# Attention phases merged by pair, one PSUM ring, and weight blocks three in flight: a sigmoid-attention and gated-MLP kernel

## The chip, the cores and the metric

The kernel runs on one core of a Trainium2 chip. It is one launch, and what counts is the device time of that launch in microseconds. Five engines work on it, each with its own instruction queue: TensorE (PE; its weight loads are shown apart as PEld), VectorE (DVE), ScalarE (ACT), GpSimd (POOL) and SyncE (SP), which here only issues transfers. PE writes its results to PSUM, eight banks of 512 fp32 words per partition; ACT and DVE read them from there.

## The reference

Attention with a sigmoid in place of the softmax, over 8 batches, 12 heads, 448 positions, 64 channels, and then a gated MLP with a spatial product, on the heads laid side by side (768 channels):

```python
scores = scale * np.matmul(q, k.transpose(0, 1, 3, 2)) - np.log(S)
attn = 1.0 / (1.0 + np.exp(-scores))
x = np.matmul(attn, v)                      # then heads side by side
h = np.maximum(x @ w_in, 0.0)
u, v = h[..., :d_ff // 2], h[..., d_ff // 2:]
v_n = (v - mean(v)) / np.sqrt(var(v) + 1e-06)
v_s = np.einsum('ts,bsd->btd', w_spatial, v_n) + b_spatial[None, :, None]
return (u * v_s) @ w_out
```

d_ff is 1024, so `u` and `v` have 512 columns. All arrays are float32, but `w_in` and `w_out` reach the chip as 64-bit words, which the kernel converts to fp32 itself.

## The kernel before

**Numbers.** Where precision is needed, an fp32 tile is split into a high and a low part (`split`, L99: a copy to fp32r, then a difference on DVE), and a product is three matmuls (`TERMS`, L217).

**Attention.** A unit is a pair of heads of one batch (`units`, L457: 48), and the loop of `attention` (L470) takes two units, an even and an odd one, called a pair below. The 448 key positions of a unit are three full tiles of 128 and 64 left over; the two leftovers of a pair share one tile, the short one. So a pair has seven tiles of scores: three even, one short, three odd. For each, `attention_scores` (L221) writes scores for two heads into two PSUM banks (`psc`), and ACT makes the sigmoid `at` of them (L254, 128x896). Full tiles have two matmuls side by side, each on half of the rows (64*128, L246); the short one has four on quarters of the array (64*64, L228). `attention_values` (L267) multiplies `at` with `v`, two matmuls side by side, each on half of the columns (128*64, L284), and sums over the tiles of a unit in one PSUM bank (`pav`); then ACT copies the sum to the high part of `x_s` (L290) and DVE makes the low part (L263). In a pair the order on PE is: short scores, even scores, odd values of the pair before, odd scores, even and short values.

**MLP.** For two batches at a time (m = 0 to 3): `gate_values` (`pv`, four groups of sequence tiles), `spatial` (`pg`), `gated` (`pu`), `output` (`po`), in the order of L526 to L554. The first scores of the next two batches stand ahead of the last three `output` calls, and `attention` goes on behind them.

**Memory that is handed round.** PSUM is three pairs of banks (`ps_2`, L82, all of `psc`, `pv`, `pg`, `pu`, `po`) and two single banks (`ps_1`, `pav`). In SBUF, the raw `q` and `k` of units and the weight blocks of the MLP share three buffers (`raw`), the splits three (`split`), `v` three (`v`). A buffer is given out in turn, and whoever takes it waits for its last reader.

**Weights.** `weight_steps` (L141) is a generator: 22 blocks (12 of `w_in`, 4 of `w_spatial`, 6 of `w_out`) are loaded, converted and split, and `load_weights(n)` (L192) runs it up to its n-th next `yield`. At m = 0 calls stand between the other work: the first 13 blocks (`NFIRST`) are done on DVE alone beside the first attention, the other nine in the MLP, by DVE and ACT in turn (sign and clamp on DVE L114 and L121, scaling on ACT L123, two joins on DVE L130 and L133, copy on ACT L178, difference on DVE L182). One block is finished before the next is begun.

**Order.** `in_program_order` (L18) keeps every engine's instructions in the order in which the code writes them, so that the place of a call is its place in each queue.

Of the kernel before, what the change touches and what calls it, by code (L numbers as in the profile page):

```python
# [8 lines left out]
F32 = mybir.dt.float32  # L9
# [5 lines left out]
P = 128  # L15
# [20 lines left out]
def attn_gmlp_kernel(  # L36
# [70 lines left out]
    YB = 4  # L107
    BIG = 7

    def convert(l, raw, scalar):  # L110

        r = raw.rearrange("p (n w) -> p w n", w=2)
        low, a = r[:, 0], r[:, 1]
        nc.vector.tensor_scalar(l, a, 0x80000000, None, op0=ALU.bitwise_and)  # L114


        af = a.bitcast(F32)
        bound = 122879.9921875
        if scalar:

            nc.vector.tensor_scalar(af, af, -bound, bound, op0=ALU.max, op1=ALU.min)  # L121
            yield
            nc.scalar.mul(af, af, 2.0**-112)  # L123
        else:
            nc.vector.tensor_scalar(
                a, a, 1, 1, op0=ALU.logical_shift_left, op1=ALU.logical_shift_right
            )
            nc.vector.tensor_scalar(af, af, bound, 2.0**-112, op0=ALU.min, op1=ALU.mult)
        yield
# [6 lines left out]
        yield  # L136

# [3 lines left out]
    def weight_steps():  # L141
# [8 lines left out]
        def load(n):  # L150
            if n < len(steps):
                src, _, i = steps[n]
                w = 512 if src is w_sp else 1024

                if n < NFIRST:
                    raw = work.tile([P, 1024], U32, tag="tmp", name=f"wraw_{n}", bufs=3)[:, :w]
                else:
                    raw = work.tile([P, 1024], U32, tag="raw", name=f"wraw_{n}", bufs=3)
# [6 lines left out]
        for n, (src, dst, i) in enumerate(steps):  # L165
# [3 lines left out]
            hi, lo = dst[:, i, 0], dst[:, i, 1]  # L169
            scalar = n >= NFIRST  # L170
            val = raws.pop(n)
            if src is not w_sp:
                raw = val
                val = work.tile([P, 512], U32, tag="wval", name=f"wval_{n}", bufs=2)
                yield from convert(val, raw, scalar)
                val = val.bitcast(F32)
            if scalar:
                nc.scalar.copy(hi, val)  # L178
                yield
            else:  # L180
                nc.vector.tensor_copy(hi, val)
            nc.vector.tensor_sub(lo, val, hi.bitcast(F32))  # L182
            if not scalar:
                yield


    NFIRST = NCC + NFC + 3
    NYIELDS = 3 * (NCC + 3) + NFC
# [10 lines left out]
    def attention_loads(b, hp):  # L199
        raw = work.tile([P, 1024], F32, tag="raw", name=f"raw_{b}_{hp}", bufs=3)[:, : 2 * S]  # L200
# [409 lines left out]
```

## Time and profile before

| | us |
|---|---|
| median of three runs | 694.8 (693.76 to 695.07) |
| the profiled execution | 694.26 |
| its span, first to last instruction | 692.5 |
| ACT busy | 249.2 |
| DVE busy | 283.9 |
| POOL busy | 18.5 |

The span is what the profile's rows add up to; the remaining 1.8 us of the execution lie around it. A row of a view has the start, the length, the engine, the line of the kernel, the operation with the tiles written and read, and how many such instructions were merged. A row of the chain of waits has the start, the length and who held the chain then. Mean granted clock of TensorE over the span is 0.997. Busy time by slices (a digit is tenths, 40 slices of 17.3 us):

```
PE   9999999989999999999999999999999999999997
DVE  2999576723243337321324414621224241553020
ACT  7887121322476601011257741010136773101111
```

The slices with ACT at 5 to 8 are the four attentions; those with ACT at 1 to 3 the MLPs between them.

### The profile page before, as it was taken

What the parts mean: (1) busy time and instruction counts of PE and PEld (TensorE: products, weight loads), DVE (VectorE), ACT (ScalarE), POOL (GpSimd) and SP (SyncE); (2) the same over time, 40 slices, a digit from 0 to 9 for tenths busy, and PEclk for the clock granted to TensorE, in tenths of its full rate; (3) what the DMA queues carried; (4) which work ended last, traced back from release to release, by engine and by line L of the source; (5) the groups of instructions that cost most, each with busy time, mean ns of one, the idle gap of its engine ahead of it and who ended that gap; (6) DMA issues with size and microseconds to landing.
All of it is one profiled execution on the core that took longest, in us unless ns stands there. A gap on an engine that the chain in (4) does not pass through costs nothing.

```text
span 692.5 us, 9010 instructions
## 1 busy us (share of the span) xinstructions
PE 684.0 (99%) x3826; PEld 501.9 (72%) x3826; DVE 283.9 (41%) x451; ACT 249.2 (36%) x299; POOL 18.5 (3%) x36
## 2 busy tenths in 40 slices
PE   9999999989999999999999999999999999999997
PEld 3454889978744478999864448899985445889996
DVE  2999576723243337321324414621224241553020
ACT  7887121322476601011257741010136773101111
POOL 0000010000000001000000000100000000110000
PEclk9999999999999999999999999999999999999999
DMA  8683111242243000005332300000433410000102
GB/s 290 224 283 123 31 36 56 87 162 80 86 155 133 1 1 0 1 4 182 107 134 85 129 1 0 1 1 27 160 129 112 158 56 0 1 1 0 54 27 80
DMA packets 20552, 55.37 MB, mean 80 GB/s; under 512 B 1952, under 2 KB 8352, under 8 KB 20512
## 3 DMA queue, kind: packets, MB, share of 16 engines
q1 hardware_dynamic: 20224, 54.57, 22.8%
q8 instruction: 30, 0.49, 0.3%
q10 hardware_dynamic: 288, 0.23, 0.1%
q14 instruction: 10, 0.08, 0.0%
HBM read 43.78 MB, written 11.01 MB: 79 GB/s over the span
## 4 chain that ended last, share of the span: by engine, by line
PE 98%; DVE 1%; ACT 0%; issue 0%; ACTq 0%
PE pav L284 20%; PE po L297 17%; PE pu L297 17%; PE pv L297 17%; PE psc L246 14%; PE pg L297 10%; PE psc L228 3%; PE warm L306 0%; DVE gs L101 0%; DVE g L416 0%; DVE osb L450 0%; ACT osb L448 0%; DVE w_out_s L182 0%; DVE wval L133 0%; DVE wval L130 0%
## 5 line engine op out<-in xcount | busy, mean ns | idle before, releaser
L254 ACT ACTIVATE at<-psc,bias_s 128x896 f32<-128x896 f32 x168 | 156.0, 1008 | 35.4 <-PE psc L228 25.3
L284 PE MATMUL pav<-at,v 128*64 128x448 f32 (+1 forms) x768 | 140.5, 551 | 0.0
L297 PE MATMUL po<-gs,w_out_s 128*128 128x448 f32 x576 | 122.5, 372 | 3.8 <-ACT w_out_s L178 2.5
L297 PEld LDWEIGHTS po<-gs,w_out_s 128*128 128x128 f32 x576 | 108.9, 190 | 16.4 <-ACT w_out_s L178 2.8
L297 PE MATMUL pu<-x_s,w_in_s 128*128 128x448 f32 x576 | 118.0, 365 | 0.0
L297 PE MATMUL pv<-w_in_s,x_s 128*128 128x512 f32 x504 | 115.4, 390 | 0.0
L297 PEld LDWEIGHTS pu<-x_s,w_in_s 128*128 128x128 f32 x576 | 108.2, 188 | 8.6
L297 PEld LDWEIGHTS pv<-w_in_s,x_s 128*128 128x128 f32 x504 | 94.3, 188 | 22.3 <-issue 2.8
L246 PEld LDWEIGHTS psc<-qks 64*128 64x128 f32 x828 | 72.3, 184 | 39.3 <-ACT at L254 17.5
L284 PEld LDWEIGHTS pav<-at,v 128*64 128x64 f32 (+1 forms) x768 | 42.0, 135 | 78.2 <-issue 73.6
L246 PE MATMUL psc<-qks 64*128 64x448 f32 x828 | 97.7, 377 | 0.0
L263 DVE TENSOR_TENSOR x_s<-pav,x_s 128x448 fp32r<-128x448 f32 x48 | 30.0, 624 | 123.3 <-ACT x_s L290 123.2
L297 PE MATMUL pg<-w_sp_s,vn 128*128 128x448 f32 x352 | 72.8, 365 | 0.0
L297 PEld LDWEIGHTS pg<-w_sp_s,vn 128*128 128x128 f32 x352 | 66.0, 187 | 5.8
L454 ACT COPY osb<-po 128x896 f32<-128x896 f32 x23 | 20.9, 908 | 117.3 <-PE po L297 106.7
L416 DVE SCALAR_TENSOR_TENSOR g<-pu,g 128x896 f32<-128x896 f32 x16 | 17.5, 1092 | 92.1 <-PE pu L297 92.1
L101 DVE TENSOR_TENSOR qks<-raw,qks 128x832 fp32r<-128x832 f32 x46 | 46.7, 1024 | 13.0 <-ACT qks L100 11.8
L100 ACT CAST gs<-g 128x896 fp32r<-128x896 f32 x12 | 11.3, 944 | 105.5 <-DVE g L416 105.5
L100 DVE CAST qks<-raw 128x832 fp32r<-128x832 f32 x36 | 21.2, 588 | 66.7 <-PE po L297 35.3
L290 ACT CAST x_s<-pav 128x448 fp32r<-128x448 f32 x48 | 25.6, 533 | 53.9 <-PE pav L284 53.5
L332 ACT ACTIVATE rv<-pv 128x1024 f32<-128x1024 f32 (+1 forms) x16 | 14.6, 915 | 81.4 <-PE pv L297 81.4
L336 DVE BATCH_NORM_STATS2 stats<-rv 128x6 f32<-128x512 f32 x28 | 19.0, 679 | 47.4 <-ACT rv L332 47.4
(41 smaller groups left out, 242.1 us busy)
## 6 DMA issues: line engine op xcount, KB each, us to landing
raw<-qk_dram SPq DMA_DIRECT2D x48, 448.0 KB, 4.3
v<-v_dram SPq DMA_DIRECT2D x24, 448.0 KB, 4.2
out_dram<-osb SPq DMA_DIRECT2D x23, 448.0 KB, 2.6
wraw<-w_in_dram SPq DMA_DIRECT2D x12, 512.0 KB, 4.2
wraw<-w_out_dram SPq DMA_DIRECT2D x6, 512.0 KB, 3.6
wraw<-w_sp_dram SPq DMA_DIRECT2D x4, 256.0 KB, 4.7
b_bc<-b_sp_dram SPq DMA_DIRECT2D x1, 256.0 KB, 5.0
out_dram<-osb ACTq DMA_DIRECT2D x2, 112.0 KB, 1.7
```

The lines of the kernel that those rows point to most:

```text
L100: copy(hi, src)
L101: nc.vector.tensor_sub(lo, src, hi.bitcast(F32))
L228: nc.tensor.matmul(psc[odd * HALF : (odd + 1) * HALF, j, :S], raw[rows, PART:], raw[rows, FULL:PART], start=True, stop=True,)
L246: nc.tensor.matmul(psc[:, j, :S], st[rows, k : k + P], mv[rows, FULL:PART], start=i == 0, stop=i == len(ops) - 1,)
L254: nc.scalar.activation(at, psc[:, :, :S], AF.Sigmoid, bias=bias_s, scale=QK)
L263: nc.vector.tensor_sub(*late.pop(0))
L284: nc.tensor.matmul(pav[heads, :S], vt[rows, t, heads], at[rows, j], start=start, stop=stop)
L290: nc.scalar.copy(x[:, 0], pav)
L297: nc.tensor.matmul(ps, st, mv, start=start and i == 0, stop=stop and i == len(ops) - 1)
L336: nc.vector.bn_stats(stats, rv[:, i])
L416: nc.vector.scalar_tensor_tensor(g, pu[:, :, :S], 0.0, g, op0=ALU.max, op1=ALU.mult)
L454: nc.scalar.copy(osb, po[:, :, :S])
```

## The change

Four things change.

1. In `attention`, a pair has one phase of scores (short, even, odd) and one of values (even, odd, short); the values of a pair no longer reach into the next one. Both units of a pair end at the short tile, and the four instructions that bring them to `x_s` stand together: two copies on ACT, then two differences on DVE.
2. PSUM becomes one ring of four pairs of banks; `pav` takes one bank of a pair for each of the two units.
3. Weights: 11 blocks in the attention instead of 13. The other eleven are worked on in three parts (`begin`: sign, clamp, scaling; `middle`: two joins, copy; the difference), and the parts of three blocks are interleaved. Of the calls of `load_weights` in the MLP the ones behind the `output` phases go, and earlier ones run more steps.
4. Buffers: `raw` four instead of three, `v` two instead of three, `wval` three instead of two; the loads of `q` and `k` are issued a unit earlier.

```diff
-    ps_2 = ctx.enter_context(tc.tile_pool(name="ps_2", bufs=3, space=bass.MemoryType.PSUM))
-    ps_1 = ctx.enter_context(tc.tile_pool(name="ps_1", bufs=2, space=bass.MemoryType.PSUM))
+    ps_2 = ctx.enter_context(tc.tile_pool(name="ps_2", bufs=4, space=bass.MemoryType.PSUM))
...
+        def begin(n):
+            low, a = words(raws.pop(n))
+            l = value(n)
+            sign(l, a)
+            a = a.bitcast(F32)
+            nc.vector.tensor_scalar(a, a, -BOUND, BOUND, op0=ALU.max, op1=ALU.min)
+            nc.scalar.mul(a, a, SCALE)
+            return l, low, a.bitcast(U32)
+
+        def middle(n, l, low, a):
+            join(l, low, a)
+            nc.scalar.copy(parts(n)[0], l.bitcast(F32))
+            return l.bitcast(F32)
+
+        begun, joined = {}, {}
+        for n in range(NFIRST, len(steps) + 2):
+            load(n + AHEAD)
+            if n < len(steps):
+                begun[n] = begin(n)
+            if n - 2 in joined:
+                hi, lo = parts(n - 2)
+                nc.vector.tensor_sub(lo, joined.pop(n - 2), hi.bitcast(F32))
+            yield
+            if n - 1 in begun:
+                joined[n - 1] = middle(n - 1, *begun.pop(n - 1))
+            yield
...
-    NFIRST = NCC + NFC + 3
-    NYIELDS = 3 * (NCC + 3) + NFC
+    NFIRST = NCC + NFC + 1
+    NYIELDS = 3 * (NCC + 1) + NFC
...
-    def attention_values(b, hp, t, at):
+    def attention_values(b, hp, ats):
         vt = values[b, hp]
...
+        pav = banks(f"pav_{b}_{hp}")
+        evens, odds = range(NFULL), range(NFULL + 1, TILES)
+        for t in (*evens, *odds, NFULL):
+            at = ats(t)
...
+                    nc.tensor.matmul(
+                        pav[heads, odd, :S],
+                        vt[rows, t, heads],
+                        at[rows, j],
+                        start=t == odd * (NFULL + 1),
+                        stop=t == NFULL,
+                    )
+        cols = slice((b % 2) * S, (b % 2 + 1) * S)
+        parts = [(x_s[:, :, hp + odd, cols], pav[:, odd, :S]) for odd in range(2)]
+        for x, ps in parts:
+            nc.scalar.copy(x[:, 0], ps)
+        for x, ps in parts:
+            nc.vector.tensor_sub(x[:, 1], ps, x[:, 0].bitcast(F32))
...
-        load_weights(2 * (n - 1))
+        load_weights(1 if ts[0] else 5)
...
-            if i == 0:
-                load_weights(n - 1)
...
-        load_weights(YB * (b % 2))
+        load_weights(2)
...
         nc.vector.scalar_tensor_tensor(g, pu[:, :, :S], 0.0, g, op0=ALU.max, op1=ALU.mult)
-        load_weights(1)
...
         ahead(attention_loads, n + 2)
+        ahead(attention_loads, n + 3)
...
         for n in range(first, end, 2):
...
+            if n:
+                scores(n, short + evens)
+            else:
+                scores(n, evens)
...
+            if n and n == first:
+                yield
+                attention_splits(*units[n + 1])
+            if n:
+                loads()
+            scores(n, odds)
+            if not n:
+                scores(n, short)
+            weigh(WEIGH + (n + 2 == end))
+            if not n:
+                loads()
             ahead(attention_splits, n + 2, end)
             ahead(attention_splits, n + 3, end)
-            vals(n, evens + short)
-            weigh(3 + (n + 2 == end))
-        vals(end - 2, odds)
+            attention_values(*units[n], lambda t: ats.pop((n, t)))
...
         output(b0, (0, 1))
-        load_weights(YB)
         output(b0, (2, 3))
-        load_weights(YB + 1)
         start_loads(m + 1)
```

`WEIGH` is 4. `value(n)` takes a buffer `wval`, `words(raw)` the two 32-bit halves of the 64-bit words, `sign` and `join` are the passes of the old `convert`.

**PE in the middle of the second attention** (batch 3, the pair of heads 2 and 3; a name is the tile, the batch, the head pair and, for scores, the key tile: 0 to 2 even, 3 short, 4 to 6 odd). Before, from the even scores on:

```order
L246 MATMUL psc_3_2_0_1858<-qks_3_2_1827 128x448 x6
L246 MATMUL psc_3_2_1_1867<-qks_3_2_1827 128x448 x6
L246 MATMUL psc_3_2_2_1876<-qks_3_2_1827 128x448 x6
L284 MATMUL pav_3_1_1842<-at_3_0_4_1807,v_3_0_1666 64x448 x2
L284 MATMUL pav_3_1_1842<-at_3_0_5_1816,v_3_0_1666 64x448 x2
L284 MATMUL pav_3_1_1842<-at_3_0_6_1825,v_3_0_1666 64x448 x2
L246 MATMUL psc_3_2_4_1893<-qks_3_3_1830 128x448 x6
L246 MATMUL psc_3_2_5_1902<-qks_3_3_1830 128x448 x6
L246 MATMUL psc_3_2_6_1911<-qks_3_3_1830 128x448 x6
L284 MATMUL pav_3_2_1926<-at_3_2_0_1865,v_3_2_1761 64x448 x2
L284 MATMUL pav_3_2_1926<-at_3_2_1_1874,v_3_2_1761 64x448 x2
L284 MATMUL pav_3_2_1926<-at_3_2_2_1883,v_3_2_1761 64x448 x2
```

PE in the changed kernel, at the same place:

```order
L269 MATMUL psc_3_2_0_1851<-qks_3_2_1817 128x448 x6
L269 MATMUL psc_3_2_1_1860<-qks_3_2_1817 128x448 x6
L269 MATMUL psc_3_2_2_1869<-qks_3_2_1817 128x448 x6
L269 MATMUL psc_3_2_4_1880<-qks_3_3_1820 128x448 x6
L269 MATMUL psc_3_2_5_1889<-qks_3_3_1820 128x448 x6
L269 MATMUL psc_3_2_6_1898<-qks_3_3_1820 128x448 x6
L295 MATMUL pav_3_2_1913<-at_3_2_0_1858,v_3_2_1784 64x448 x2
L295 MATMUL pav_3_2_1913<-at_3_2_1_1867,v_3_2_1784 64x448 x2
L295 MATMUL pav_3_2_1913<-at_3_2_2_1876,v_3_2_1784 64x448 x2
L295 MATMUL pav_3_2_1913<-at_3_2_4_1887,v_3_2_1784 64x448 x2
L295 MATMUL pav_3_2_1913<-at_3_2_5_1896,v_3_2_1784 64x448 x2
L295 MATMUL pav_3_2_1913<-at_3_2_6_1905,v_3_2_1784 64x448 x2
```

The odd values of the pair before have left their place between the even and the odd scores, and each pair's odd values stand behind its even ones.

**ACT at the same place,** from the last sigmoid of the pair before on. Before:

```order
L254 ACTIVATE at_3_0_6_1825<-psc_3_0_6_1818,bias_s_72 128x2x448
L290 CAST x_s_71<-pav_3_0_1833 128x448
L254 ACTIVATE at_3_2_3_1852<-psc_3_2_3_1847,bias_s_72 128x2x448
L254 ACTIVATE at_3_2_0_1865<-psc_3_2_0_1858,bias_s_72 128x2x448
L254 ACTIVATE at_3_2_1_1874<-psc_3_2_1_1867,bias_s_72 128x2x448
L254 ACTIVATE at_3_2_2_1883<-psc_3_2_2_1876,bias_s_72 128x2x448
L290 CAST x_s_71<-pav_3_1_1842 128x448
L254 ACTIVATE at_3_2_4_1900<-psc_3_2_4_1893,bias_s_72 128x2x448
```

ACT in the changed kernel:

```order
L277 ACTIVATE at_3_0_6_1815<-psc_3_0_6_1808,bias_s_69 128x2x448
L305 CAST x_s_68<-pav_3_0_1823 128x448 x2
L277 ACTIVATE at_3_2_3_1849<-psc_3_2_3_1844,bias_s_69 128x2x448
L277 ACTIVATE at_3_2_0_1858<-psc_3_2_0_1851,bias_s_69 128x2x448
L277 ACTIVATE at_3_2_1_1867<-psc_3_2_1_1860,bias_s_69 128x2x448
L277 ACTIVATE at_3_2_2_1876<-psc_3_2_2_1869,bias_s_69 128x2x448
L277 ACTIVATE at_3_2_4_1887<-psc_3_2_4_1880,bias_s_69 128x2x448
```

Both copies to `x_s` now stand ahead of the short tile's sigmoid, and none between the even and the odd ones.

**ACT in the MLP of m = 0,** from the second `gated` of b = 0 to its `output` copies (L454 before; `wraw_19` and `wval_19` are parts of block 19 of the weights). Before:

```order
L100 CAST gs_0_2_1120<-g_0_2_1020 128x896
L178 CAST w_out_s_68<-wval_17_1113 128x512
L123 ACTIVATE wraw_18_1060<-wraw_18_1060 128x512
L178 CAST w_out_s_68<-wval_18_1150 128x512
L123 ACTIVATE wraw_19_1111<-wraw_19_1111 128x512
L178 CAST w_out_s_68<-wval_19_1185 128x512
L454 COPY osb_0_0_1195<-po_0_0_1194 128x2x448
L123 ACTIVATE wraw_20_1148<-wraw_20_1148 128x512
L178 CAST w_out_s_68<-wval_20_1223 128x512
L454 COPY osb_0_2_1231<-po_0_2_1230 128x2x448
L123 ACTIVATE wraw_21_1183<-wraw_21_1183 128x512
L178 CAST w_out_s_68<-wval_21_1259 128x512
```

ACT in the changed kernel:

```order
L98 CAST gs_0_2_1136<-g_0_2_1034 128x896
L188 ACTIVATE wraw_21_1076<-wraw_21_1076 128x512
L193 CAST w_out_s_65<-wval_20_1127 128x512
L193 CAST w_out_s_65<-wval_21_1139 128x512
L467 COPY osb_0_0_1203<-po_0_0_1202 128x2x448
L467 COPY osb_0_2_1231<-po_0_2_1230 128x2x448
L467 COPY osb_0_4_1269<-po_0_4_1268 128x2x448
```

The last two blocks, 20 and 21, stood between the copies of the first batch's `output` phases; now all weights stand ahead of the first of them.

More of the change, by code (lines that the diff above doesn't have):

```diff
@@ L135, in convert @@
         )
-        yield
     AHEAD = 2
@@ L157, in load @@
                 else:
-                    raw = work.tile([P, 1024], U32, tag="raw", name=f"wraw_{n}", bufs=3)
+                    raw = work.tile([P, 1024], U32, tag="raw", name=f"wraw_{n}", bufs=4)
                 raws[n] = raw.bitcast(F32) if src is w_sp else raw
@@ L164, in weight_steps, with value, parts @@
         yield
-        for n, (src, dst, i) in enumerate(steps):
+        def value(n):
+            return work.tile([P, 512], U32, tag="wval", name=f"wval_{n}", bufs=3)
+        def parts(n):
+            _, dst, i = steps[n]
+            return dst[:, i, 0], dst[:, i, 1]
+        for n, (src, dst, i) in enumerate(steps[:NFIRST]):
             load(n + AHEAD)
@@ L199, in attention_loads @@
     def attention_loads(b, hp):
-        raw = work.tile([P, 1024], F32, tag="raw", name=f"raw_{b}_{hp}", bufs=3)[:, : 2 * S]
+        raw = work.tile([P, 1024], F32, tag="raw", name=f"raw_{b}_{hp}", bufs=4)[:, : 2 * S]
         nc.sync.dma_start(raw, qk[b, hp])
@@ L204, in value_loads @@
     def value_loads(b, hp):
-        vt = work.tile([P, 2 * NFULL + 1, P], F32, tag="v", name=f"v_{b}_{hp}", bufs=3)
+        vt = work.tile([P, 2 * NFULL + 1, P], F32, tag="v", name=f"v_{b}_{hp}", bufs=2)
         nc.sync.dma_start(vt, v[b, hp // 2])
@@ L255, in attention_scores @@
         return at
-    pav_of = {}
-    late = []
-    def late_splits():
-        while late:
-            nc.vector.tensor_sub(*late.pop(0))
-    last = (NFULL, TILES - 1)
-    def attention_values(b, hp, t, at):
-        vt = values[b, hp]
-        for odd in range(2):
-            if t == NFULL:
-                rows = slice(odd * HALF, (odd + 1) * HALF)
-            elif (t > NFULL) == odd:
-                rows = slice(0, P)
-            else:
-                continue
-            unit = b, hp + odd
-            start = t == odd * NFULL
-            stop = t == last[odd]
-            if start:
-                pav_of[unit] = ps_1.tile([P, 512], F32, tag="ps1", name=f"pav_{b}_{hp + odd}")
-            pav = pav_of[unit]
-            for j in range(2):
-                heads = slice(j * D, (j + 1) * D)
-                nc.tensor.matmul(pav[heads, :S], vt[rows, t, heads], at[rows, j], start=start, stop=stop)
-        for odd in range(2):
-            if t == last[odd]:
-                sl = slice((b % 2) * S, (b % 2 + 1) * S)
-                x = x_s[:, :, hp + odd, sl]
-                pav = pav_of.pop((b, hp + odd))[:, :S]
-                nc.scalar.copy(x[:, 0], pav)
-                late.append((x[:, 1], pav, x[:, 0].bitcast(F32)))
```

78 lines of the change are left out of this document (31 added, 47 removed).

## The prediction

> **What bounds the kernel now.** I read the head of the page, then the chain of waits in order of time, then the timeline of one pair of units, and last the busy times by stage.
>
> ```profile
> PE 684.0 (99%) x3826; PEld 501.9 (72%) x3826; DVE 283.9 (41%) x451; ACT 249.2 (36%) x299; POOL 18.5 (3%) x36
> PE 98%; DVE 1%; ACT 0%; issue 0%; ACTq 0%
> ```
>
> TensorE (PE) is busy 684.0 of 692.5 us and carries 98% of the chain that ended last. So an edit pays only where it shortens PE's own sequence or removes one of the few gaps. The largest gap is in the chain of waits, in the MLP of the first batch pair (m = 0), where the first `output` phase meets weights that are not converted yet. The last row is the same phase at m = 1:
>
> ```profile
> 130.49 9.87 PE po L297 x48
> ...
> 141.23 0.66 ACT wraw L123
> ...
> 141.91 0.70 DVE wval L130
> ...
> 144.02 0.70 DVE w_out_s L182
> ...
> 144.76 5.28 PE po L297 x17
> ...
> 304.64 14.78 PE po L297 x72
> ```
>
> The reader is to see one block of `w_out` going from ACT to DVE and on, one step after the other, while PE stands. The phase takes from 130.49 to 144.76 + 5.28 = 150.04, so 19.55 us, against 14.78 for the same matmuls later: **4.77 us lost**. The second place is attention, which has the same beat all through. One period of it:
>
> ```profile
> 24.47 0.75 PE psc L228 x8
> 25.22 2.09 PE psc L246 x18
> 27.31 2.41 PE pav L284 x12
> 29.71 2.02 PE psc L246 x18
> 31.73 3.32 PE pav L284 x20
> 35.05 0.75 PE psc L228 x8
> ```
>
> 35.05 - 24.47 = 10.58 us for a pair of units: short scores, even scores, odd values of the pair before, odd scores, even and short values. PE never stops, but it changes its tile shape at every border, and the borders cost something:
>
> ```profile
> 214.90 1.58 PE L246 MATMUL psc<-qks 64*128 64x448 f32 x14
> 216.11 0.36 PE L246 MATMUL psc<-qks 64*128 64x448 f32 x2
> ```
>
> These are rows of PE's timeline, cut so that it begins at two different matmuls of one scores phase. Two matmuls side by side make a step; six steps lie between the two starts, so a step of scores is (216.11 - 214.90) / 6 = 0.202 us. A step of the 64-column kind is 0.75 / 2 = 0.375, from the short scores above, whose eight matmuls run four abreast; values step at the same beat. The scores phase of 18 matmuls has 9 steps, 1.82 us, and takes 2.02: 0.20 for going in and out. The values phase of 12 has 6 steps, 2.25, and takes 2.41: 0.16.
>
> **The change part by part.**
>
> *Merging the phases.* A pair now has one scores phase and one values phase, so one entry and exit of each goes: 0.20 + 0.16 = 0.36 us. In the first pair of each attention the scores stay cut in two by the outputs, so five borders of six go: 5 x 0.36 = 1.8 us for each m. The number of matmuls does not change.
>
> *The new wait.* The values' accumulator now lies in the ring of four pairs of banks. Per pair the ring gives out eight: short, three even, three odd, values. So values gets the banks of the third even tile, and the next pair's third even tile gets those of values. These are free only when both copies (ACT) and both differences (DVE) have read them, and both units end together, at the short tile. Rows for this, 209.02 being the start of the short scores:
>
> ```profile
> 209.02 0.93 PE L228 MATMUL psc<-raw 64*64 64x448 f32 x8
> 209.24 0.53 ACT L290 CAST x_s<-pav 128x448 fp32r<-128x448 f32 x1 [1.66 <-PE pav L284]
> 209.80 0.62 DVE L263 TENSOR_TENSOR x_s<-pav,x_s 128x448 fp32r<-128x448 f32 x1 [1.57 <-ACT x_s L290]
> 210.11 3.70 ACT L254 ACTIVATE at<-psc,bias_s 128x896 f32<-128x896 f32 x4 [0.34 <-PE psc L228]
> 211.17 0.50 PEld L246 LDWEIGHTS psc<-qks 64*128 64x128 f32 x6 [0.18 <-ACT at L254]
> 33.30 1.68 ACT L100 CAST qks<-raw 128x832 fp32r<-128x832 f32 x2
> 24.10 1.95 DVE L101 TENSOR_TENSOR qks<-raw,qks 128x832 fp32r<-128x832 f32 x2
> ```
>
> Counted from the short scores: first copy at 0.22. The last two rows bound what two alike behind each other do: two casts of about 0.90 take 1.68, two differences of 1.02 take 1.95, so they overlap by about 0.1. Second copy from 0.65 to 1.18; the first difference stands behind both copies (one event is counted for the two), from 1.21, the second ends at about 1.21 + 0.54 + 0.62 = 2.37, and PE can load its weights 0.05 later, at 2.42. In the profile before, the third even tile's weights load at 211.17 - 209.02 = 2.15. **So PE waits 0.28 us** that it does not wait now. Bounds: nothing, if the banks come free by 2.15; with no overlap anywhere and twice the event delays 0.22 + 1.06 + 0.10 + 1.24 + 0.10 = 2.72, so 0.57. I take 0.28, since each piece has a row of its own.
>
> Net, per merged pair: 0.36 - 0.28 = 0.08 us; 20 of them, 1.6 us. The end of each attention gains about 0.1 more, since the odd values of the last pair no longer stand as a phase of their own behind the short ones: 0.4. Attention: **-2.0 us**, between 20 x 0.36 = 7.2 gained and 20 x 0.21 = 4.2 lost.
>
> *ACT's place.* Seven tiles now arrive in a row, one in 0.6 us, and ACT clears one in 3.70 / 4 = 0.92 (0.90 start to start). Its first sigmoid moves from 1.09 to about 1.12, behind the second copy. Odd tile k waits for sigmoid k, and these end at 2.1, 3.0, 3.9 where PE wants the banks at 3.0, 3.6, 4.2. Values wait for the fourth sigmoid, which ends at 1.12 + 3 x 0.90 + 1.01 = 4.83; PE is there at 5.0. So ACT hides, by 0.2 us. Were the wait of 0.28 not there, ACT would hold PE at about 4.9 and give back 0.15 of the gain.
>
> A rule speaks against this part. The Trainium skill, "TensorEngine Tiling (Array Packing)", section Performance Considerations, says that tiling speeds up TensorE but not the evacuation of PSUM, whose copies may become the bottleneck. The trace bears it out in that ACT's 0.90 a tile is slower than PE's 0.6 in this phase; it would bind PE only by the 0.15 just given, and over a whole period ACT has time.
>
> ```profile
> 5.00:69.20 64.20, 64.20 (x445) 29.83 (x441) 52.68 (x92) 52.62 (x63) 0.00 (x0) 1.00 0.66 231
> 69.20:98.00 28.80, 28.80 (x129) 23.86 (x128) 17.44 (x35) 5.98 (x9) 2.32 (x4) 1.00 0.12 37
> 98.00:107.10 9.10, 9.10 (x46) 8.25 (x45) 7.42 (x16) 1.74 (x3) 2.26 (x4) 1.00 0.21 59
> 107.10:121.70 14.60, 14.60 (x74) 13.54 (x73) 9.21 (x14) 2.90 (x4) 0.00 (x0) 1.00 0.11 36
> 121.70:130.50 8.80, 8.80 (x45) 8.26 (x45) 7.89 (x12) 2.85 (x4) 0.00 (x0) 1.00 0.26 73
> 130.50:150.00 19.50, 16.78 (x73) 14.69 (x73) 10.91 (x18) 5.46 (x8) 0.00 (x0) 0.91 0.46 164
> 182.60:243.40 60.80, 60.80 (x432) 29.44 (x431) 20.71 (x29) 42.01 (x50) 0.00 (x0) 1.00 0.26 91
> ```
>
> These are busy times by stage: length, then PE, weight loads, DVE, ACT, POOL, granted clock, DMA share, GB/s. In attention ACT has 42.0 of 60.8 us, and in the first attention 52.6 of 64.2, so it catches up within the period.
>
> *Weights at m = 0.* Two blocks fewer are converted during the first attention, where DVE has 52.7 of 64.2 us; that frees it and moves nothing on PE. Eleven instead of nine are converted in the MLP, each begun two calls before it is finished, so that the round from DVE to ACT and back lies beside other work, and the last is finished ahead of the first `output`. On DVE a block costs two short passes, two joins and one difference:
>
> ```profile
> L114 DVE TENSOR_SCALAR wval<-wraw 128x512 uint32<-128x512 uint32 x18 | 7.6, 424 | 0.0
> L121 DVE TENSOR_SCALAR wraw<-wraw 128x512 f32<-128x512 f32 x9 | 3.9, 431 | 0.3
> ```
>
> 0.42 + 0.43 + 3 x 0.70 = 2.95 us. Between 69.2 and 130.5 DVE is busy 17.44 + 7.42 + 9.21 + 7.89 = 42.0 of 61.3 us, with about six and a half blocks in it. With all eleven it would be 42.0 + 4.5 x 2.95 = 55.3. That fits, but with 6 us to spare. In DVE's own order the split of the second `gated` of b = 0, which the first `output` reads after its sixth matmul, then ends about 1 us before PE wants it; the last two blocks have 10 us more, since only the third `output` reads them. So I count **the whole 4.77 us as gone**, with 0.5 to 2.5 returning if DVE slips by its spare. What hides the conversions is PE's 61.3 us of products.
>
> *The rest.* Loads of `q` and `k` come a unit earlier and with four buffers instead of three; values have two buffers instead of three. Transfers land 4.2 to 4.3 us after issue by the page's list of DMA issues, and each is issued about 10 us or more ahead of its reader, so I cost it at nothing; uncovered, a late `v` would hold the values phase and also the two raw loads behind it on SP's queue.
>
> **Sum,** against the profiled execution's own time of 694.26 us (span 692.5; the median of the runs shown is 694.8, half a microsecond above): 694.26 - 4.77 - 2.0 = **687.5 us**.
>
> **The rivals.** (A) The banks come free in time, because copies and differences go faster than I add up. Then ACT's 0.15 is the only loss: 20 x 0.21 = 4.2 in place of 1.6, 684.9 us. For it: the overlaps of 0.1 us are read off longer instructions. Against: DVE cannot start before 1.2. (B) The release takes its upper bound, or DVE slips in the MLP: 20 x 0.2 lost in place of 2.0 gained, or 2.5 us returned, 690 to 692. For it: 6 us of spare on an engine that waits for ACT in between. (C) The weights do not come in time after all, so that the change does not do what it says: attention alone is left, 692.3. Against: the last block stands ahead of the `output` in the order. (D) Slower: DVE reaches the two differences late, because the splits of the next units stand ahead of them in its queue and wait for a late transfer. Each us then costs PE a us in every period. From 0.35 us late the 20 periods eat all gains (20 x 0.35 = 7); at 0.8 late 16 us are lost, 703. Against: 20.7 of 60.8 us are DVE's, and it is free at about 5.6 of 10.6. (E) PE's new short waits lower its clock. In the profile 0.91 of the clock was granted in the stage with 4 us of gap (130.50 to 150.00), 1.00 where PE waited 0.18 in each period, so I hold it for unlikely; with 3.4 us at half clock in each of 20 periods it would be 20 x 1.7 = 34 us more, about 721. The Trainium skill, "TensorE: Matmul & The Clock Gate", section "A second HAM failure mode: psum-queue depth-cycling", tells of such a loss from small idle times between groups; no run here shows it so far.
>
> **How the numbers follow.** Forecast 0.50 (686 to 689.5), A 0.20 (683 to 686), B 0.18 (689.5 to 692.5), C and whatever else ends near no change 0.05, D 0.05, E 0.02. The range leaves out D, E, C and the far ends of A and B: 683.0 to 691.5. A measurement of this kernel can tell about 0.2% (1.4 us) from no change: faster 0.88, same 0.05, slower 0.07.
>
> **What would show it.** The first `output` at m = 0 should take 14.8 us without a gap, and the clock stay at 1.00 there. A period of attention should be 10.5 us, with PE's weight load for the third even tile waiting about 0.3 us on the difference of `x_s`. The forecast is wrong if that wait is over 0.6 us, if the values phase waits for a sigmoid, or if PE waits in the m = 0 MLP for `gs` or a weight block.

## The result, and the profile after

| | before | changed |
|---|---|---|
| median | 694.49 us (693.76 to 695.07, four runs) | 690.64 us (690.43 to 690.91, four runs) |
| the profiled execution, its span | 694.26, 692.5 | 690.91, 689.1 |
| mean granted clock | 0.997 | 1.000 |

The ratio of the changed kernel to the one before is 0.9945, with a 95% interval of 0.9928 to 0.9963: it is faster, by 3.4 us between the spans and 3.9 between the medians. The forecast was 687.5 us, 6.8 below the profiled execution. The time is inside the range (683.0 to 691.5), but in the band of rival B (689.5 to 692.5) and not in that of the forecast.

(One execution of a kernel below, the profiled one of *attn*, ran at a granted clock of 0.752 over its whole span and took 843.09 us; it is compared with nothing, and *attn_again* is a second profile of that kernel.)

The head of the page, and the share of the engines in the chain that ended last, after the change:

```profile
PE 677.9 (98%) x3826; PEld 508.2 (74%) x3826; DVE 280.6 (41%) x447; ACT 245.8 (36%) x303; POOL 18.5 (3%) x36
PE 92%; DVE 4%; ACT 3%; issue 1%
```

PE's busy time fell by 6.1 us, the span by 3.4 only. DVE and ACT, which had 1% of the chain together, now have 7%: PE has less to do and waits more. The chain of waits of the changed kernel (start, length, who held it), at the second pair of m = 0, at the first `output` phase, and over one period of the second attention:

```profile
15.50 0.98 ACT x_s L305 x2
16.48 1.95 DVE qks L99 x2
18.43 1.08 DVE x_s L307 x2
...
27.99 0.98 ACT x_s L305 x2
...
70.51 28.80 PE pv L313 x126
...
131.78 14.78 PE po L313 x72
...
208.06 0.98 ACT x_s L305 x2
...
209.06 1.17 DVE x_s L307 x2
210.23 0.14 issue
210.36 2.70 PE psc L269 x24
213.06 5.62 PE pav L295 x32
...
218.71 0.98 ACT x_s L305 x2
```

Four things are to be seen. The first `output` phase takes 14.78 us, where it took 19.55. A period of attention is 218.71 - 208.06 = 10.65 us, where it was 10.58. In every period the chain leaves PE for the two copies on ACT and the two differences on DVE, and comes back to PE at the scores. And the first product `pv` of m = 0 starts at 70.51, where it started at 69.23 (the end of the window of the first attention, 69.20, in the prediction). So the account by stages is: -4.77 in the first `output`, +1.28 in the first attention; in each later m, the stretch from the first odd scores to `pv` is 0.17 longer (60.91 after 60.74), and the one ahead of it, from the first short scores over the last `output` calls to the odd scores, 0.11 shorter (17.91 after 18.02), so 3 x 0.06. The sum is -3.3 us, for -3.4 measured between the spans.

The timeline of one pair in the changed kernel (the number in brackets is idle time ahead, with what ended it), with the short scores starting at 218.46:

```profile
218.46 0.93 PE L251 MATMUL psc<-raw 64*64 64x448 f32 x8
...
219.71 1.16 DVE L307 TENSOR_TENSOR x_s<-pav,x_s 128x448 fp32r<-128x448 f32 x2 [6.37 <-ACT x_s L305]
...
220.98 2.39 PEld L269 LDWEIGHTS psc<-qks 64*128 64x128 f32 x24 [0.56 <-PE psc L269]
221.01 2.74 PE L269 MATMUL psc<-qks 64*128 64x448 f32 x24 [0.21 <-DVE x_s L307]
```

The second difference ends at 219.71 + 1.16 = 220.87, 2.41 us after the short scores began, and the weights of the third even tile are loaded at 220.98, 2.52 after. The prediction had 2.37 and 2.42.

Two stages by windows (columns as in the prediction: length, PE, weight loads, DVE, ACT, POOL, clock, DMA share, GB/s), the first `output` and the second attention:

```profile
131.70:146.60 14.90, 14.90 (x75) 13.62 (x74) 6.63 (x10) 3.65 (x5) 0.00 (x0) 1.00 0.29 91
179.10:239.90 60.80, 59.78 (x431) 31.21 (x431) 19.61 (x28) 39.92 (x49) 0.00 (x0) 1.00 0.32 107
```

PE is busy all through the first `output`, at full clock. In the second attention it has 1.0 us of idle time that the same stretch did not have before (60.80 of 60.80). That is less than the periods lose, because the rows of the last matmuls ahead of a wait reach into it (idle 0.21 us above); the periods are the better measure.

**The second pair of m = 0** was not in the prediction. The first weight instruction on DVE, and then the rows of PE:

```profile
11.48 0.43 DVE L116 TENSOR_SCALAR wval<-wraw 128x512 uint32<-128x512 uint32 x1 [10.30 <-DMA wraw<-w_in_dram]
```

```profile
17.55 1.28 PE L269 MATMUL psc<-qks 64*128 64x448 f32 x10 [0.97 <-DVE qks L99]
19.64 2.71 PE L269 MATMUL psc<-qks 64*128 64x448 f32 x24 [0.81 <-DVE x_s L307]
```

DVE waits 10.3 us for the first weight block, has nine instructions on weights from 11.48 on, and only at 16.48 (in the chain above) makes the low parts of the second pair's `q` and `k`, and after these, at 18.43, the differences that free the banks. The block had been issued at 3.04, so 8.4 us passed until it was read; the page's median for such a block was 4.2 us before and is 5.8 us now. PE is idle for 0.97 us at the even scores and for 0.81 at the third even tile, and this pair takes 27.99 - 15.50 = 12.49 us instead of 10.65. In the kernel before, DVE's order at this place was the other way round:

```profile
12.94 1.96 DVE L101 TENSOR_TENSOR qks<-raw,qks 128x832 fp32r<-128x832 f32 x2 [11.77 <-ACT qks L100]
...
15.35 0.42 DVE L114 TENSOR_SCALAR wval<-wraw 128x512 uint32<-128x512 uint32 x1
```

The splits stood ahead of the weights and were done at 14.90. The change had moved the first call of `weigh` past them.

### The profile page after: what moved, and what is told of

Read it like the earlier page. It is cut to its first block, busy times and chain, and to the rows that moved or that the text cites. A ratio compares the mean times of both kernels' runs of the same rounds, so it can differ in the third digit from the quotient of the medians.

```text
span 689.1 us, 9062 instructions
## 1 busy us (share of the span) xinstructions
PE 677.9 (98%) x3826; PEld 508.2 (74%) x3826; DVE 280.6 (41%) x447; ACT 245.8 (36%) x303; POOL 18.5 (3%) x36
## 4 chain that ended last, share of the span: by engine, by line
PE 92%; DVE 4%; ACT 3%; issue 1%
PE pav L295 20%; PE pu L313 17%; PE po L313 17%; PE pv L313 17%; PE pg L313 10%; PE psc L269 10%; DVE x_s L307 3%; ACT x_s L305 3%; PE psc L251 1%; PE warm L322 0%; DVE qks L99 0%; DVE gs L99 0%; DVE g L430 0%; DVE osb L463 0%; ACT osb L461 0%
## 5 line engine op out<-in xcount | busy, mean ns | idle before, releaser
L277 ACT ACTIVATE at<-psc,bias_s 128x896 f32<-128x896 f32 x168 | 154.3, 1032 | 23.0 <-PE psc L251 18.6
L295 PE MATMUL pav<-at,v 128*64 128x448 f32 (+1 forms) x768 | 135.4, 548 | 0.0
L313 PE MATMUL po<-gs,w_out_s 128*128 128x448 f32 x576 | 120.4, 368 | 1.0 <-DVE osb L463 0.9
L295 PEld LDWEIGHTS pav<-at,v 128*64 128x64 f32 (+1 forms) x768 | 44.2, 135 | 80.5 <-issue 73.3
L269 PEld LDWEIGHTS psc<-qks 64*128 64x128 f32 x828 | 77.8, 184 | 31.9 <-PE psc L269 11.6
L307 DVE TENSOR_TENSOR x_s<-pav,x_s 128x448 fp32r<-128x448 f32 x48 | 27.8, 620 | 135.8 <-ACT x_s L305 135.8
L305 ACT CAST x_s<-pav 128x448 fp32r<-128x448 f32 x48 | 23.2, 536 | 76.0 <-PE pav L295 76.0
```

The costliest lines, as they stand in the source:

```text
L269: nc.tensor.matmul(psc[:, j, :S], st[rows, k : k + P], mv[rows, FULL:PART], start=i == 0, stop=i == len(ops) - 1,)
L277: nc.scalar.activation(at, psc[:, :, :S], AF.Sigmoid, bias=bias_s, scale=QK)
L295: nc.tensor.matmul(pav[heads, odd, :S], vt[rows, t, heads], at[rows, j], start=t == odd * (NFULL + 1), stop=t == NFULL,)
L305: nc.scalar.copy(x[:, 0], ps)
L307: nc.vector.tensor_sub(x[:, 1], ps, x[:, 0].bitcast(F32))
L313: nc.tensor.matmul(ps, st, mv, start=start and i == 0, stop=stop and i == len(ops) - 1)
```

## The experiments

The theory after reading the two traces: the weight part takes away exactly the 4.77 us of the first `output`; merging the phases saves what was predicted, but the new wait for the banks that the copies and differences free eats all of it; and in m = 0 a burst of weight conversions ahead of the splits costs about 2 us more. Rivals: the sigmoids on ACT hold PE, not the banks; the borders between phases are worth less than counted; the loss in m = 0 comes from the loads.

All ratios are to the kernel before, measured beside it on the same chip; its medians were 693.78 to 694.49 us. Medians of two rows can come from different chips, so tenths between them mean little; where a tenth matters, it is read from the profiles.

| run | what | median, us | ratio, 95% interval |
|---|---|---|---|
| the change | | 690.64 | 0.9945 (0.9928 to 0.9963) |
| weights | before + weight part | 689.83 | 0.9939 (0.9925 to 0.9952) |
| attn | change without weight part | 696.59 | 1.0036 (1.0024 to 1.0048) |
| attn_again | the same | 698.25 | 1.0061 (1.0042 to 1.0079) |
| staged | change, banks freed by one ACT copy | 684.94 | 0.9868 (0.9855 to 0.9882) |
| onecopy | change, one copy and one difference | 686.67 | 0.9892 (0.9878 to 0.9907) |
| inter | change, copy, difference, copy, difference | 700.78 | 1.0096 (1.0081 to 1.0111) |
| twopools | change, PSUM pools of before | 700.04 | 1.0084 (1.0069 to 1.0099) |
| wlate | change, first weight call moved | 692.03 | 0.9971 (0.9959 to 0.9982) |
| behind1 | change, all weight calls moved | 689.55 | 0.9933 (0.9919 to 0.9946) |
| behind | staged and behind1 together | 683.83 | 0.9853 (0.9837 to 0.9870) |

### The two halves of the change: weights, attn, attn_again

*weights* is the kernel before with the new `weight_steps`, the calls of `load_weights` as in the change, and its buffers. In the attention the places of the calls stay, with other counts, and the loads of `q` and `k` are issued where they were before:

```diff
-                weigh(3)
+                weigh(2)
...
-            weigh(3 + (n + 2 == end))
+            weigh((4 if n < 2 else 2) + (n + 2 == end))
```

> The kernel before with the weight part of the change alone (three blocks in flight, two blocks fewer in the first attention, four raw buffers, two value buffers); phases and PSUM pools as before. If the 4.77 us in the first output phase are all that the weight part is worth: 694.3 - 4.8 = 689.5 us, the first output phase 14.8 us at clock 1.00. Rival: the weight part also costs time in the first attention, because its first block now stands ahead of the splits of the second pair in DVE's order: then 690.5 to 691.5, and the values of m=0 start up to 1.3 us later than before. If the merged phases were the source of the whole gain, 694.

Its chain of waits in m = 0:

```profile
19.11 6.63 DMA raw<-qk_dram
...
70.83 28.79 PE pv L322 x126
...
132.09 14.78 PE po L322 x72
```

689.83 us, 0.6% faster. The first `output` takes 14.78 us, as in the change. The rival's 1.3 us in the first attention is there too (`pv` at 70.83 instead of 69.23), but not for its reason: DVE makes the second pair's splits at 13.03, ahead of the weights, and the chain goes through a load of `q` and `k` that was issued only at 19.11, behind a weight load that went out at 18.26. In this mix, then, a load is late that the change, which issues these loads a unit earlier, has in time. So in the profiled execution, the slowest of the five (690.67), 4.8 us were gained and 1.6 lost again.

*attn* is the changed kernel with the old `weight_steps`, its calls, and 13 blocks in the first attention.

```diff
-    WEIGH = 4
+    WEIGH = 5
...
-    NFIRST = NCC + NFC + 1
+    NFIRST = NCC + NFC + 3
```

> The changed kernel with the old weight code (one phase of scores and one of values per pair, ring of four pairs of banks; weights converted as before). If the wait for the banks eats what a merge saves (about 0.45 us of wait against 0.36 saved), attention is no faster than before: 690.7 + 4.8 = 695.5 us, so 0.1 to 0.3% slower than before, the gap of 4.8 us back in the first output phase. By the prediction's sum (wait 0.28): 692.3. If the mode changes were dearer than counted and the m=0 loss comes from the new weight code: 691 to 692.

696.59 us, slower than before by 0.24 to 0.48%. The merged phases and the ring alone do not pay; by the prediction's sum they should have given 2.0 us. It is 1.1 us above the 695.5 expected, and where that lies is asked of a second profile:

> The same kernel as in the run attn (the change without its weight part), for a profile of its stages. attn took 696.6 where 690.7 + 4.8 = 695.5 was expected, 1.1 more. If the missing 1.1 lies in the first attention (two more weight blocks in DVE's bursts ahead of the splits): values of m=0 to the first product 71.5 to 72 us where the changed kernel has 70.5, the first output phase 19.5, the attentions of m of 1 to 3 as in the changed kernel, 60.9 from the odd scores to the product. Rival: the first output phase alone loses more (20.6), or the attentions of m of 1 to 3 do.

```profile
43.19 8.11 DMA wraw<-w_in_dram
...
73.44 28.76 PE pv L289 x126
...
134.67 9.87 PE po L289 x48
...
148.96 5.29 PE po L289 x17
```

The first `output` runs from 134.67 to 154.25, 19.58 us, so no more is lost there than before. `pv` starts at 73.44, 2.9 later than in the changed kernel and 1.4 later than the expectation allowed. The span of this execution is 696.8, 7.7 above the changed kernel's: 2.9 + 4.8. In this execution the extra lies in the first attention alone, and here the chain goes through a weight block that landed late, with the splits and the differences behind it in DVE's queue. It is an execution of 698.56 us; the five of *attn* took 695.74 to 697.00, so where the 1.1 us of *attn* lie is not shown by it, and why the same program took 1.7 us more the second time stays open.

### The wait for the banks: staged, onecopy, inter

*staged* frees the banks with one instruction in m = 1 to 3; in m = 0 it has one copy and one difference for the pair:

```diff
-        parts = [(x_s[:, :, hp + odd, cols], pav[:, odd, :S]) for odd in range(2)]
-        for x, ps in parts:
+        x, ps = x_s[:, :, hp : hp + 2, cols], pav[:, :, :S]
+        if b > 1:
+            o = work.tile([P, 2, 512], F32, tag="tmp", name=f"o_{b}_{hp}", bufs=3)[:, :, :S]
+            nc.scalar.copy(o, ps)
+            split(x[:, 0], x[:, 1], o, nc.vector.tensor_copy)
+        else:
             nc.scalar.copy(x[:, 0], ps)
-        for x, ps in parts:
             nc.vector.tensor_sub(x[:, 1], ps, x[:, 0].bitcast(F32))
```

> The changed kernel, but ACT copies values' accumulator of both units in one instruction of 128x896 to SBUF for m of 1 to 3, and DVE makes both parts from there, so that the banks are free after one ACT copy; for m=0 one copy and one difference of 128x896. If the chain of two copies and two differences sets the third even tile: that tile no longer waits, the copy ends about 1.1 us after the short scores' start instead of 2.4, and a period of m of 1 to 3 goes from 10.65 to 10.2 to 10.3 us (ACT then holds PE by 0.1): 15 such periods, 5 to 6 us less, 685 us. Rival 1: ACT's sigmoids hold PE anyway (values wait for the fourth): period 10.5 or more, 688.5 or more. Rival 2: the wait is no loss, because PE catches up in it what it loses elsewhere: no change, 690.5.

A period of it in the chain of waits:

```profile
195.96 0.75 PE psc L251 x8
196.72 3.90 PE psc L269 x36
...
200.63 5.64 PE pav L295 x32
206.28 0.75 PE psc L251 x8
```

684.94 us, as the theory had it. The chain stays on PE: the 36 scores take 3.90 in one piece, and a period is 206.28 - 195.96 = 10.32 us. Values are 5.57 long where nothing holds them (the rows of *onecopy* next), so up to 0.1 of the period is ACT holding PE at the values, and the bare period is 0.75 + 3.90 + 5.57 = 10.22. This gives both terms of the sum apart, to a few hundredths, since it adds rounded rows. **A merged pair without a wait is 10.58 - 10.22 = 0.36 us shorter than before**, the prediction's value. **The wait for the banks costs 10.65 - 10.22 = 0.43**, against 0.28 predicted.

Two more readings are needed to say what is in these numbers. One is when the weight load of the third even tile starts where nothing holds it. In *staged*, with the short scores at 206.09:

```profile
206.09 0.93 PE L251 MATMUL psc<-raw 64*64 64x448 f32 x8
...
206.96 3.58 PEld L269 LDWEIGHTS psc<-qks 64*128 64x128 f32 x36 [0.71 <-PE pav L295]
```

The 36 loads of the scores run through without a gap, six to a tile; the 13th, the first of the third even tile, starts at 208.08, 1.99 us after the short scores. In the kernel before it was 2.15, because there the load was itself held 0.18 us for a sigmoid (the row at 211.17 in the prediction). The other is that this small wait costs PE about 0.08 us a period in the kernel before: its even scores take 2.10 us, but 2.02 in the first pair of the second attention, which has no such wait:

```profile
165.54 2.02 PE psc L246 x18
```

*onecopy* shortens the chain without leaving it:

```diff
-        for x, ps in parts:
-            nc.scalar.copy(x[:, 0], ps)
-        for x, ps in parts:
-            nc.vector.tensor_sub(x[:, 1], ps, x[:, 0].bitcast(F32))
+        x, ps = x_s[:, :, hp : hp + 2, cols], pav[:, :, :S]
+        nc.scalar.copy(x[:, 0], ps)
+        nc.vector.tensor_sub(x[:, 1], ps, x[:, 0].bitcast(F32))
```

> The changed kernel with one copy and one difference of 128x896 per pair in place of two of 128x448 each. If the third even tile waits for the end of this chain: the copy takes 0.91 and the difference 1.09 in one piece against two that overlap by 0.1, with one wait between engines as before; the banks are free 2.25 us after the short scores' start instead of 2.41, so 0.15 us less per pair: 15 pairs of m of 1 to 3 give 2.3, and m=0 gains the 1.0 us that the kernel with the SBUF copy showed there with this form: 687.4 us. Rival: the wait is set by something else at that place (the sigmoid of the short scores, which moves earlier by little): 689.9 to 690.6.

Its chain over one period, and its timeline, with the short scores at 206.68:

```profile
196.40 0.75 PE psc L251 x8
...
201.28 5.57 PE pav L295 x32
206.86 0.75 PE psc L251 x8
```

```profile
207.86 1.09 DVE L305 TENSOR_TENSOR x_s<-pav,x_s 128x896 fp32r<-128x896 f32 x1 [6.24 <-ACT x_s L304]
...
209.01 2.33 PEld L269 LDWEIGHTS psc<-qks 64*128 64x128 f32 x24 [0.36 <-DVE x_s L305]
```

686.67 us, 0.7 better than expected. The chain ends at 207.86 + 1.09 = 208.95, 2.27 after the short scores' start; the 0.14 gained there was expected (2.25). The rest was not: the weights load 0.06 after the difference ends, where in the change they load 0.11 after it. So a period is 206.86 - 196.40 = 10.46 us, 0.19 less than the change's, and not 0.15 (over all periods of m = 1 to 3 the means are 10.44 and 10.66).

*inter* lengthens the chain, by deleting one line:

```diff
         for x, ps in parts:
             nc.scalar.copy(x[:, 0], ps)
-        for x, ps in parts:
             nc.vector.tensor_sub(x[:, 1], ps, x[:, 0].bitcast(F32))
```

> The changed kernel with copy, difference, copy, difference in this order in place of two copies and two differences; nothing else. If the chain that frees the banks sets the third even tile, it now runs one step after the other: banks free 2.63 us after the short scores' start or later instead of 2.41, and the sigmoid of the short scores moves from 1.1 to 1.9: 0.2 to 0.45 us more in each of 21 periods, 695 to 700 us. Rival: PE waits there for something else, or the time is made up later in the period: 690.6.

```profile
189.51 0.54 ACT x_s L305
...
191.94 0.14 issue
192.07 2.83 PE psc L269 x24
194.92 5.69 PE pav L295 x32
200.63 0.54 ACT x_s L305
```

700.78 us, 10 more than the change, a little over the expected end. The four steps (only the first is shown) now run strictly one after the other, 191.94 - 189.51 = 2.43 us instead of 210.23 - 208.06 = 2.17. A period is 200.63 - 189.51 = 11.12, so 0.47 more than the change: 0.26 is the chain, and 0.20 the scores and values behind it (2.83 + 5.69 instead of 2.70 + 5.62), which fits that the sigmoids start later too. With a shorter chain, a longer chain, and none, PE's time follows the chain each time; that the banks set the third even tile is shown.

### What the fourth pair of banks is for: twopools

```diff
-    ps_2 = ctx.enter_context(tc.tile_pool(name="ps_2", bufs=4, space=bass.MemoryType.PSUM))
+    ps_2 = ctx.enter_context(tc.tile_pool(name="ps_2", bufs=3, space=bass.MemoryType.PSUM))
+    ps_1 = ctx.enter_context(tc.tile_pool(name="ps_1", bufs=2, space=bass.MemoryType.PSUM))
...
-        pav = banks(f"pav_{b}_{hp}")
+        pavs = [ps_1.tile([P, 512], F32, tag="ps1", name=f"pav_{b}_{hp + odd}") for odd in range(2)]
```

> The changed kernel with the PSUM pools of before: three pairs of banks for scores, two single banks for values; phases merged as in the change. If ACT's 0.90 us a tile against PE's 0.6 is what the fourth pair of banks covers: the odd scores wait for sigmoids, a period takes about 11.1 us, and 20 periods cost 9 us more, 699.6 us. Rival: the ring's wait for values' banks is dearer than three pairs of score banks: faster than the change, 688 to 690.

```profile
189.28 2.10 PE psc L270 x18
191.40 0.88 PE psc L270 x6
...
200.39 2.10 PE psc L270 x18
```

700.04 us, as expected. The even scores go through in 2.10 us, but an odd tile takes 0.88 instead of 0.6: PE goes at the pace of ACT's sigmoids (0.90 a tile). A period is 200.39 - 189.28 = 11.11 us, longer than before (10.58): without the ring, merging would have cost 0.5 a pair. The ring brings it to 10.65, its wait included.

### The first attention: wlate, behind1, behind

*wlate* moves the first weight call behind the splits and values of the first pair:

```diff
-            weigh(WEIGH + (n + 2 == end))
-            if not n:
+            if n:
+                weigh(WEIGH + (n + 2 == end))
+            else:
                 loads()
...
             attention_values(*units[n], lambda t: ats.pop((n, t)))
+            if not n:
+                weigh(WEIGH)
```

> The changed kernel with the first call of weight conversion in m=0 moved behind the splits and values of the first pair. If PE's two stalls in the second pair of m=0 (about 1.2 us at the even scores, 1.0 at the third even tile) come from a weight block that arrives late and stands ahead of the splits and differences in DVE's order: the values of m=0 start 1.3 to 2 us sooner, 689.0 us (688.6 to 689.4). Rival: they come from the raw loads themselves: no change, 690.6. Other rival: the blocks are then missing later (w_in for the first gate values): 690.6 or more.

692.03 us: missed, and on the side of its rivals. Its chain of waits shows why (the profiled execution is the fastest of the six, 691.24):

```profile
15.41 0.98 ACT x_s L305 x2
...
17.57 0.34 DVE wval L116
...
27.46 1.95 DVE qks L99 x2
...
39.00 0.98 ACT x_s L305 x2
```

The second pair no longer waits: its differences are done by 17.57, ahead of the weights. But now two calls stand behind each other, and DVE converts from 17.57 to past 26.8, ahead of the splits of the third pair (27.46) and of the differences that free its banks. The stall had moved by one pair and grown: the second and third pair together take 39.00 - 15.41 = 23.59 us, 2.3 more than two regular periods, where the change lost 1.84. Neither rival is what the chain shows: there is no load of `q` and `k` in it here, and `pv` follows the last values without a wait for a block. So the theory was made sharper: it is not this call's place, but that every call stands ahead of splits. *behind1* moves all of them:

```diff
-    WEIGH = 4
+    WEIGH = 5
...
-            weigh(WEIGH + (n + 2 == end))
...
             attention_values(*units[n], lambda t: ats.pop((n, t)))
+            weigh(WEIGH)
```

> The changed kernel with the weight calls of m=0 alone moved behind each pair's splits, values and differences, five calls over five pairs; two copies and two differences as in the change. If the burst ahead of the splits is what the second pair of m=0 loses: that stall of about 2 us goes, the first pair pays 0.5 as it did with the SBUF copy, 1.3 to 1.6 us less than the change: 689.2 us (688.9 to 689.5), and the attentions of m of 1 to 3 stay at 60.9 us. Rival: without the shorter chain for the banks DVE is too late in every pair of m=0: 690.6 or more, as with the first call moved alone.

```profile
16.09 0.98 ACT x_s L305 x2
...
26.74 0.98 ACT x_s L305 x2
...
69.26 28.80 PE pv L313 x126
```

689.55 us, 0.05 above the expected range. The second pair now takes 26.74 - 16.09 = 10.65 us, the period of all others, where it took 12.49 in the change. The first pair ends 0.59 later, so `pv` starts 1.25 us earlier, at 69.26, and the span is 1.1 less (688.0). By medians against before the intervals of this kernel and of the change overlap; the 1.25 us are read from the profiles.

*behind* puts the same edit on *staged*:

> The kernel with the SBUF copy (staged: 684.9 us, measured), but in m=0 each pair converts its weights behind its own splits and differences, five calls a pair over five pairs, in place of four ahead of them over six. Moving the first call alone only moved the stall to the next pair. If a burst of conversions (5 us on DVE) ahead of the splits is what the first attention loses: each pair has its splits done in time, the 1.8 us stall of the second pair goes and its period of m=0 is 10.4 us, 682.6 us (682 to 684). Rivals: DVE (9.3 of 10.4 us a period) doesn't keep up, or the blocks then miss the first gate values: 685 or more; the loads hold the pairs: 685.

683.83 us, 1.1 under *staged* and at the upper end of what was expected, which had not counted the 0.6 of the first pair. It is 1.5% faster than the kernel before (1.30 to 1.63%) and the fastest of this study.

## Why the prediction was right or wrong

- **The first `output`, 4.77 us gone: right,** in size and place. 14.78 us without a gap at clock 1.00, in the change and in *weights* alone; back to 19.58 in *attn_again*. DVE's room in the MLP was enough: no wait for `gs` or a weight block is left in the chain there. Not all of the 4.77 was standing, though: in the prediction's row of that stage PE is busy 16.78 of 19.50 us, so 2.7 were idle, and the same 72 products took 2.0 longer than the 14.78 of later, in a stage with a granted clock of 0.91. How much of these 2.0 is the clock's was not tried.
- **0.36 us saved for each merged pair: the size right, in part by luck** (10.58 - 10.22, from *staged*). Some 0.08 of it is the small wait for a sigmoid that the period before had and *staged* has not. The borders alone gave about 0.3: 0.16 at the values, as predicted (2.41 + 3.32 became 5.57), and 0.14 at the scores, where 0.20 was predicted (2 x 2.02 became 3.90).
- **The new wait, 0.28 us: the mechanism right, the size wrong.** This is the term of the sum that was mis-sized: 0.43 us, inside its bounds (0 to 0.57). The chain of copies and differences came within 0.04 of the working (2.41 after 2.37). Two things were missed. From the difference's end to the weight load it is 0.11 and not 0.05 (in *onecopy*, with one difference in place of two, 0.06); that makes the load 2.52 instead of 2.42. And the prediction counted the wait from 2.15, where the load stood before, as if PE wanted the banks only then; but 2.15 held a wait already, and without one the load comes at 1.99 (*staged*). Counted from 2.15, the load is 0.37 late; the 0.08 that the earlier wait cost PE come on top, which gives the 0.43 within 0.02. With 0.36 saved and 0.43 paid, a merge loses 0.07 instead of gaining 0.08; over m = 1 to 3, 1.7 us of the forecast went this way (3 x 0.06 lost in place of 3 x 0.5 gained).
- **ACT hides at the values: right** in the change. Where the wait is taken away (*staged*), ACT holds PE by 0.1 us a period; the prediction had 0.15. The rule of the Trainium skill that was weighed ("TensorEngine Tiling (Array Packing)", section Performance Considerations: evacuating PSUM may become the bottleneck) agrees with what the runs show: PE's time is set here by how fast ACT and DVE clear PSUM, in the change by the accumulator of values (2.41 us for its chain), in *twopools* by the score tiles (0.88 us a tile). It reached PE by the accumulator, not by the sigmoids against which it had been weighed.
- **Two blocks fewer in the first attention: "that frees it and moves nothing on PE". This step failed.** It cost 1.84 us in the second pair of m = 0 (12.49 - 10.65). The working looked at DVE's load over the whole stage (52.7 of 64.2 us before, and less to come), which says nothing of order. In the code of the change `weigh` stands ahead of `attention_splits` in the first pair, and the first block, which is issued behind four loads of `q` and `k` now, is there only at 11.48 us; everything on DVE waits behind it. Rival D had this mechanism (differences late because of what stands ahead of them on DVE, behind a late transfer), but for splits and for all periods; it happened once, with weights. *behind1* gave 1.25 of it back. How much the late landing does, and how much the burst by itself, was not tried apart. An estimate from rows: the nine instructions take 5.0 us (11.48 to 16.48), and without them the splits begin at 13.03 (*behind1*), so a block that had landed by 8.0 would have been done in time.
- **The loads, at nothing:** right in the change, whose PE waits for none of them behind the first pair. *weights* shows that they have little to spare: 1.6 us were lost in its profiled execution to one load of `q` and `k`. The landing time of 4.2 to 4.3 us, a median, did not hold at the start, where the first weight block was read 8.4 us after its issue.
- **Rival B: its time, not its mechanism.** The measured time lies in its band, but neither did the release take its upper bound of 0.57, nor did DVE slip in the MLP; a wait of 0.43 and a stall in the first attention added up to it, and that is luck. Its band is also added up too low: 20 x 0.2 lost in place of 2.0 gained is 693.5, and not 692.
- **Rival E, the clock:** no execution of the change had it. It was granted 1.00 with a wait of 0.43 us in each of 20 periods. The loss of which the Trainium skill tells ("TensorE: Matmul & The Clock Gate", section "A second HAM failure mode: psum-queue depth-cycling") was not seen here in any run of the change.

So of the 6.8 us forecast, 4.8 came; the 2.0 of attention turned into a loss of 1.5, half of it (1.8 of 3.5) in one pair of m = 0 and half in the steady wait for the banks. The first half is shown by *behind1*, the second by *staged*, *onecopy* and *inter*.

## What to carry to other kernels

When an accumulator moves into the ring that feeds the next phase, write down the whole chain that frees it, each engine's turn and the restart of PE too, and compare it with the time until the ring comes round; here 0.43 us of wait undid the 0.36 us that a merge saved, and a plain copy to SBUF by one engine (10.32 instead of 10.65 us a period) made the change worth 1.3% instead of 0.55%. An engine with free time over a stage can still be late: background work must stand in its queue behind what PE needs next, and a load that it waits for counts as work. Take a gain apart before believing its explanation: the weight half alone gave as much as the whole change, and the attention half alone was slower than before.

## What the runs showed of the hardware that was not expected

- PE's weight load behind a wait for DVE started 0.11 us after the last difference in the change (220.87 to 220.98), and 0.06 after it in *onecopy* (208.95 to 209.01); the chain shows it as 0.14 of "issue" in the change and in *inter*. In the change's trace an instruction of PE's own queue that only waits for a semaphore of DVE lies in between (220.90, 0.05 us long; the same at 210.26 in the period before), and the load behind it waits for a second semaphore, which PE's matmuls raise. In *onecopy* there is no such instruction at that place, and the load waits for DVE's semaphore alone. This agrees with the Trainium skill, "Perfetto Trace Analysis", section Identifying Dependency Chains: an instruction that waits on several engines may get such instructions ahead of it, with the additional waits. Why one kernel has the second wait and the other has not, the runs do not show.
- The first loads take much longer than the median. In the change the first weight block was issued at 3.04 us and read at 11.48, with seven more loads issued between 0.72 and 4.8; the page's median from issue to landing is 5.8 us for these blocks.
